# First expert tile's rows gathered into the tile of the diagonal's blocks, and a second list built in smaller pieces

## The chip, the cores and the metric

The kernel runs on one core of a Trainium2 chip. The metric is the device time of one launch in microseconds (us). Engines are named as in the profile: PE (TensorE's matmuls; PEld its weight loads), DVE (VectorE), ACT (ScalarE), POOL (GpSimd) and SP (the queue that starts most DMAs). Each engine works through its own queue in order, so a waiting instruction holds all that stand behind it.

## The reference

Attention without a softmax (the scaled scores pass through a relu and are squared), gated by u, is followed by a mixture of eight experts in which each token goes to its best one:

```python
B, S, D = 8, 2496, 256                   # d_qk = 64
scores = (1.0 / S) * np.matmul(z, z.transpose(0, 2, 1))
attn = np.maximum(scores, 0.0) ** 2
x = (u * np.matmul(attn, v)).reshape(B * S, D)
logits = x @ w_gate                      # E = 8
expert_idx = np.argmax(logits, axis=1)
probs = np.exp(logits - logits.max(-1, keepdims=True))
probs /= probs.sum(-1, keepdims=True) + 1e-09
gate_w = probs[np.arange(N), expert_idx]
for e in range(E):
    mask = expert_idx == e
    h = np.maximum(x[mask] @ w1[e], 0.0)     # F = 1024
    out[mask] = gate_w[mask, None] * (h @ w2[e])
```

## The kernel before

**Attention.** Eight batches of 2496 positions, each in five chunks of columns (four of 512, the last of 448), and each chunk in ten steps, `steps`. For a step, `scores()` makes two blocks of scores (it runs three steps ahead), and `weighted()` multiplies them with v into the chunk's accumulators. Values are carried as a high and a low part, which ACT and DVE make (`thi`, `tlo`). The matrix of scores is symmetric. Blocks on the diagonal go through a tile called `sd`, of which there is one; PE's transposes (line 298) are its last reads in a chunk. The last chunk of a batch (448 columns) doesn't use it.

**At a chunk's end.** `gate_x` multiplies with u and puts pieces on a list of background work, `bg`, of which one is issued at each following step (and later at each group of a tile): `logits` (its two small transposes `lg<-lp`, line 391, go out on SP), `turn_rows` (four transposes `rows<-th`, line 372, on SP, into a buffer of the ring `rows`, three deep), two empty turns, and then the three of `route`: `choose` (line 420 reads the transposed logits on DVE), `exps`, and `place`, which computes each token's place within its expert's list, stores the chunk's rows to memory (`xrows<-rows`, line 462) and scatters token numbers to the lists (`lst<-toks`, four indirect DMAs on POOL, line 467).

**Experts.** Tokens are handled in tiles of at most 512 rows, all of one expert. Six tiles (the list `la`, "A") hold tokens of the first seven batches and are known well before attention ends; the others (the list `lf`, "F") are made by `tile_list` after the last chunk, whose pieces stand on `bg` too. For each tile i: `load_w` fetches weights (POOL, line 672), `load_x` gathers the tile's rows, with a gate weight behind each row, by four indirect DMAs on POOL (line 681) into a buffer of the ring `rows`; `turn_x` transposes them by four DMAs on SP into `th` (line 712) and copies the four gate weights out, on DVE (line 714, `gt<-rows`); `split_x` makes the high and low parts, on ACT (lines 723 and 726) and DVE (724 and 727); `split_piece` does the same for the weights (lines 701 to 704). Then come 8 groups of a tile: `up` (line 744), a relu on ACT (line 748) and its low part on DVE (line 749), and `down` (lines 765 and 767), 14 matmuls in a full tile's group. `up` runs two groups ahead. In a tile's last group `finish` scales by the gate and scatters the rows out (lines 776 to 779). While tile i runs, the next ones are made ready: `load_x(i + 3)` at its first group, `turn_x(i + 2)` at its middle one, `split_x(i + 1)` three from its end.

**What sets the order.** A table, `loads`, says at which step, counted back from attention's last, the first tiles' loads, gathers and turnings are issued. A scheduler then orders each engine's queue by its own estimate of times; work issued through `pinned` stands behind the last instruction that each engine has been given so far. The table before:

```python
loads = {NKP + 4: [lambda: load_w(0, 0), lambda: load_w(0, 1)],
         NKP + 3: [lambda: load_x(0)],
         NKP - 1: [lambda: load_w(1, 0)],
         NKP - 4: [lambda: load_x(1)],
         NKP - 5: [lambda: turn_x(0)],
         1: [lambda: load_x(2)],
         0: [lambda: turn_x(1)]}          # NKP = 10
```

## Time and profile before

| | |
|---|---|
| runs | 2364.37, 2366.27, 2368.11 us (median 2366.27) |
| profiled execution | 2356.92 us, its span 2355.2 us |
| PE busy | 2303.9 us, 98% of the span |
| DVE busy | 1649.2 us, 70% |
| ACT busy | 1423.5 us, 60% |
| POOL busy | 641.6 us, 27% |

A row of the timeline gives the start, the duration, the engine, the line and what is written from what; in brackets stand the engine's idle time ahead of the row and what released it. "DMA rows<-xrows" as a releaser means that the engine waited for that transfer to land. A row of the windows gives, for a stretch, how long each engine was busy in it, the granted clock of PE (1.00 is full speed), and what the DMA engines did. Times are counted from the span's start. Attention ends and the experts begin near 1420 us.

### The profile page before, as it was taken

How to read it: one execution, taken by the hardware profiler on the slowest of the kernel's cores; microseconds unless marked ns; L12 is line 12 of the kernel's file. 1: busy time of each engine (PE TensorE's matmuls, PEld its weight loads, DVE VectorE, ACT ScalarE, POOL GpSimd, SP SyncE). 2: the span in 40 equal slices, each digit the busy share in tenths (PEclk: the TensorE clock that was granted, in tenths of full speed). 3: DMA queues.
4: the chain of work that ended last, by engine and by line, in shares of the span. 5: the costliest groups of instructions: out<-in, count | busy, mean ns of one | idle time of the engine just before them, and what ended most of it. 6: DMA issues, size and time to landing. Idle time of an engine off the chain costs nothing. (4 is left out here: it accounts for less than half of the span.)

```text
span 2355.2 us, 32513 instructions
## 1 busy us (share of the span) xinstructions
PE 2303.9 (98%) x11636; PEld 1937.7 (82%) x11636; DVE 1649.2 (70%) x3078; ACT 1423.5 (60%) x1944; POOL 641.6 (27%) x639
## 2 busy tenths in 40 slices
PE   8999999999999999999999988999999999999998
PEld 6888887888888888887888876788888888888887
DVE  8868868868868868868868846655666557557554
ACT  6757648658658648648658644355555556556443
POOL 4111111111111111111111225345445445346322
PEclk9999999999999999999999999999999999999999
DMA  5636637747647547547546767465657647557620
GB/s 136 102 65 120 114 62 121 109 68 133 103 69 139 88 78 135 91 74 131 98 75 115 126 114 130 115 150 166 170 140 193 148 133 198 149 147 190 148 87 28
DMA packets 424921, 280.16 MB, mean 119 GB/s; under 512 B 358380, under 2 KB 381690, under 8 KB 415536
## 3 DMA queue, kind: packets, MB, share of 16 engines
q1 hardware_dynamic: 393360, 158.91, 38.7%
q0 software_dynamic: 31392, 119.10, 18.5%
q8 instruction: 93, 1.52, 0.3%
q14 instruction: 76, 0.62, 0.1%
HBM read 149.79 MB, written 43.43 MB: 82 GB/s over the span
## 5 line engine op out<-in xcount | busy, mean ns | idle before, releaser
L332 PE MATMUL acc<-thi,t 128*128 128x512 f32 (+1 forms) x1600 | 619.9, 388 | 0.0
L329 PE MATMUL acc<-thi,t 128*128 128x512 f32 (+1 forms) x1600 | 595.7, 391 | 5.8 <-DVE thi L303 5.6
L331 PE MATMUL acc<-tlo,t 128*128 128x512 f32 (+1 forms) x1520 | 590.7, 389 | 4.3 <-DVE tlo L305 3.4
L765 PE MATMUL y<-t,t 128*128 128x512 f32 x1062 | 384.7, 399 | 4.5 <-ACT t L748 4.5
L749 DVE SCALAR_TENSOR_TENSOR t<-ph,t 128x512 fp32r<-128x512 f32 (+1 forms) x328 | 221.1, 675 | 235.0 <-ACT t L748 232.6
L744 PE MATMUL ph<-thi,t 128*128 128x512 f32 (+2 forms) x1248 | 379.9, 362 | 0.9 <-ACT thi L726 0.9
L467 POOL DMA_INDIRECT lst<-toks,posi x160 | 190.8, 1193 | 640.7 <-DVE posi L459 573.2
L748 ACT ACTIVATE t<-ph 128x512 fp32r<-128x512 f32 (+1 forms) x328 | 192.0, 588 | 279.6 <-PE ph L744 274.8
L329 PEld LDWEIGHTS acc<-thi,t 128*128 128x128 f32 x1600 | 300.9, 189 | 60.1 <-DVE thi L303 6.8
L332 PEld LDWEIGHTS acc<-thi,t 128*128 128x128 f32 x1600 | 301.8, 189 | 55.6
L331 PEld LDWEIGHTS acc<-tlo,t 128*128 128x128 f32 x1520 | 287.1, 189 | 58.7 <-DVE tlo L305 7.2
L767 PE MATMUL y<-t,t 128*128 128x256 f32 x1062 | 297.0, 283 | 10.8 <-DVE t L749 10.8
L744 PEld LDWEIGHTS ph<-thi,t 128*128 128x128 f32 x1248 | 227.3, 190 | 39.5 <-ACT thi L726 1.3
L765 PEld LDWEIGHTS y<-t,t 128*128 128x128 f32 x1062 | 200.8, 189 | 49.0 <-ACT t L748 4.9
L744 PE MATMUL ph<-tlo,t 128*128 128x512 f32 (+2 forms) x624 | 225.9, 362 | 0.8 <-DVE tlo L727 0.8
L767 PEld LDWEIGHTS y<-t,t 128*128 128x128 f32 x1062 | 202.3, 190 | 21.6 <-DVE t L749 12.6
L779 POOL DMA_INDIRECT out_dram<-tf,lfidx x136 | 143.3, 1054 | 276.5 <-DVE tf L777 246.6
L293 PE MATMUL ps_s<-t,t 128*128 128x512 f32 (+1 forms) x480 | 179.0, 377 | 0.0
L301 ACT ACTIVATE tf<-ps_s 128x1024 f32<-128x1024 f32 (+2 forms) x129 | 116.8, 906 | 92.2 <-PE ps_s L293 45.5
L681 POOL DMA_INDIRECT rows<-xrows,lfidx x136 | 141.3, 1039 | 44.1 <-issue 39.2
L303 DVE CAST thi<-tf 128x1024 fp32r<-128x1024 f32 (+2 forms) x129 | 85.1, 660 | 82.8 <-ACT tf L302 78.4
L267 DVE TENSOR_TENSOR tlo<-ps_s,thi 128x896 fp32r<-128x896 f32 (+1 forms) x80 | 89.1, 1114 | 61.4 <-ACT thi L266 60.9
(250 smaller groups left out, 3999.9 us busy)
## 6 DMA issues: line engine op xcount, KB each, us to landing
vr<-in_v_dram SPq DMA_DIRECT2D x80, 256.0 KB, 2.9
xrows<-rows SPq DMA_DIRECT2D x32, 544.0 KB, 3.9
u<-in_ut_dram SPq DMA_DIRECT2D x32, 512.0 KB, 4.5
zr<-in_zt_dram SPq DMA_DIRECT2D x40, 256.0 KB, 5.0
u<-in_ut_dram SPq DMA_DIRECT2D x8, 448.0 KB, 5.4
xrows<-rows SPq DMA_DIRECT2D x8, 408.0 KB, 3.6
rows<-th SPq DMA_TRANSPOSE x160, 4.7
lst<-toks,posi POOLq DMA_INDIRECT x160
```

The lines of the kernel that those rows point to most:

```text
L293: nc.tensor.matmul(ps[:, i, m:n], lhsT=hl_k, rhs=lh_q[:, m:n], start=False, stop=True)
L329: nc.tensor.matmul(acc[d][:, :n], lhsT=vh, rhs=hi[:, i, :n], start=first and i == 0, stop=False)
L331: nc.tensor.matmul(acc[d][:, :n], lhsT=vh, rhs=lo[:, i, :n], start=False, stop=False)
L332: nc.tensor.matmul(acc[d][:, :n], lhsT=vl, rhs=hi[:, i, :n], start=False, stop=last and i == 1)
L467: i = nc.gpsimd.indirect_dma_start(out=lst1, out_offset=bass.IndirectOffsetOnAxis(ap=posi[:m, j:j + 1], axis=0), in_=toks[:m, col + j:col ...
L681: nc.gpsimd.indirect_dma_start(out=xg[:, s, :], out_offset=None, in_=src, in_offset=bass.IndirectOffsetOnAxis(ap=lists[which]["idx"][:, s, ...
L744: nc.tensor.matmul(o, lhsT=w1[:, part, dd, fs], rhs=xx[:, dd, :n], start=p == 0, stop=p == 5)
L748: nc.scalar.activation(hh[:, :m], ph[:, :m], AF.Relu)
L749: nc.vector.scalar_tensor_tensor(hl[:, :m], ph[:, :m], 0.0, hh[:, :m].bitcast(F32), op0=ALU.max, op1=ALU.subtract)
L765: nc.tensor.matmul(y, lhsT=hh[:, cs], rhs=w2[:, f % 2].rearrange("p i d -> p (i d)"), start=f == 0, stop=False)
L767: nc.tensor.matmul(y[:, 0:D], lhsT=hl[:, cs], rhs=w2[:, f % 2, 0, :], start=False, stop=f == NF - 1)
L779: d = nc.gpsimd.indirect_dma_start(out=out, out_offset=bass.IndirectOffsetOnAxis(ap=lists[which]["idx"][:, s, t:t + 1], axis=0), in_=yo[:, ...
```

## The change

- The first tile's rows are gathered into the tile `sd`, which gets the shape of a `rows` buffer for that (`ring_sd`), in place of a buffer of the ring `rows`.
- `turn_x` loses the copy of the gates; that is a function of its own, `take_gates`.
- The table `loads` is new: tile 0 is gathered 12 steps from attention's end (13 before), tile 1 at 11 (6), tile 2 at 6 (1); tile 0 is turned at 9 (5) and tile 1 at 5 (0); their gates are copied at 7 and 3. All of these but the weights' pieces are `pinned`.
- Behind the last chunk's `turn_rows` stand four empty turns in place of two, so its `choose`, `exps` and `place` come two groups later.
- The second list is made in 15 pieces in place of 9; the first one's pieces stay as they were.
- In the tiles' loop the loads of weights are written under other conditions; POOL gets them in the order in which it got them.

```diff
+    def ring_sd():
+        return sb.tile([P, QC // P, ROW], I32, name="sd", tag="sd")
...
-            a = stored[b, c, c] = sb.tile([P, 2, QC], F32, name="sd", tag="sd")
+            sd = ring_sd().bitcast(F32).rearrange("p s r -> p (s r)")[:, 0:2 * QC]
+            a = stored[b, c, c] = sd.rearrange("p (i n) -> p i n", i=2)
...
-        bg.extend([nothing] * 2 + route(b * S + q0, n, ns, lg, xr))
+        bg.extend([nothing] * (4 if b == B - 1 and c == NC_ - 1 else 2) + route(b * S + q0, n, ns, lg, xr))
...
-        return r, [count] + ([middle, others] if ns else []) + [experts, rows, nothing, nothing, lambda: places(0), lambda: places(1)]
+        def all_of(*some):
+            return [lambda: [f() for f in some]]
+
+        if not ns:
+            return r, ([count] + all_of(lambda: experts(parts), experts2) + all_of(rows, rows2) + [nothing, nothing] +
+                       [lambda: places(0), lambda: places(1)])
+        nbig = t("nbig")
+        return r, [count, middle, middle2, lambda: others([(0, nd, 2 * BS, ndbl)]),
+                   lambda: others([(1, nb, BS, nbig)]), remaining, lambda: experts(parts[:2]),
+                   lambda: experts(parts[2:]), experts2, rows, rows2, nothing, nothing,
+                   lambda: places(0), lambda: places(1)]
...
-        xg = ring_rows()
+
+        xg = ring_sd() if i == 0 else ring_rows()
...
-        gates[i] = sb.tile([P, BS], F32, name="gt", bufs=4)
-        nc.vector.tensor_copy(gates[i][:, 0:k], xgs.pop(i)[:, 0:k, D].bitcast(F32))
-        turned[i] = tp
+        turned[i] = tp
+
+    def take_gates(i):
+        gates[i] = sb.tile([P, BS], F32, name="gt", bufs=4)
+        nc.vector.tensor_copy(gates[i][:, 0:blocks[i]], xgs.pop(i)[:, 0:blocks[i], D].bitcast(F32))
...
-             NKP + 3: [lambda: load_x(0)],
...
-             NKP - 5: [lambda: turn_x(0)],
-             1: [lambda: load_x(2)],
-             0: [lambda: turn_x(1)]}
+             NKP + 2: [lambda: load_x(0)],
+             NKP + 1: [lambda: load_x(1)],
+             NKP - 1: [lambda: load_w(1, 0), lambda: turn_x(0)],
+             NKP - 3: [lambda: take_gates(0)],
+             NKP - 4: [lambda: load_x(2)],
+             NKP - 5: [lambda: turn_x(1)],
+             NKP - 7: [lambda: take_gates(1)]}
...
-            f()
+            f() if f in plain else pinned(f)
...
-                for w, h in ((wof[i] + 1, 1), (wof[i] + 2, 0)):
-                    if own[i] and w <= wof[hi - 1]:
+                for w, h in ((wof[i] + 1, 0), (wof[i] + 1, 1), (wof[i] + 2, 0)):
+                    if own[i] and w <= wof[hi - 1] and (w, h) not in weights and (w < NA or i > NA):
...
                 turn_x(i + 2)
+                take_gates(i + 2)
```

Line numbers move: 681 becomes 706, 712 becomes 737, 714 is 742, 723 and 724 are 750 and 751, 744 is 771, 748 and 749 are 775 and 776, 462 is 466, 467 is 471, 391 is 395, 372 is 376, 420 is 424, 253 is 256, 267 is 270, 303 is 307, 388 is 392.

**VectorE at the last chunk's steps, before.** `gt` are the gate weights that are copied out, here tile 1's; `thi` and `tlo` are the two parts of scores or rows, line 702 is a weight's low part, and lines 388 and 389 write the logits of the chunk before.

```order
L267 TENSOR_TENSOR tlo<-ps_s,thi 128x2x448
L704 TENSOR_TENSOR t_13524<-s_13124,t_13524 128x2x256
L714 COPY gt<-rows 128x4
L702 TENSOR_TENSOR t_13552<-s_13124,t_13552 128x512
L267 TENSOR_TENSOR tlo<-ps_s,thi 128x2x448
L388 COPY lp<-lt 16x512
L389 COPY lp<-lt 16x512
```

**and now:**

```order
L270 TENSOR_TENSOR tlo<-ps_s,thi 128x2x448
L729 TENSOR_TENSOR t_13536<-s_13124,t_13536 128x2x256
L727 TENSOR_TENSOR t_13559<-s_13124,t_13559 128x512
L270 TENSOR_TENSOR tlo<-ps_s,thi 128x2x448
L742 COPY gt<-sd 128x4
L392 COPY lp<-lt 16x512
L393 COPY lp<-lt 16x512
L270 TENSOR_TENSOR tlo<-ps_s,thi 128x2x448
L372 COPY th<-x 128x1024
L729 TENSOR_TENSOR t_13560<-s_13124,t_13560 128x2x256
L751 COPY x<-th 128x1024
```

Tile 1's copy has left this place, and tile 0's, out of `sd`, has come to it from a place ahead of the last full chunk's split of the diagonal's block (lines 303 and 305). Tile 1's now stands further on, with tile 2's, around the reading of the logits of the chunk before the last:

```order
L313 TENSOR_TENSOR tlo<-tf,thi 128x448
L314 TENSOR_TENSOR thi<-tf,thi 64x448
L270 TENSOR_TENSOR tlo<-ps_s,thi 128x2x448
L742 COPY gt<-rows 128x4
L424 COPY lw<-lg 128x64 x2
L742 COPY gt<-rows 128x4
L727 TENSOR_TENSOR s_13775<-s_13318,s_13775 128x512
L729 TENSOR_TENSOR s_13775<-s_13318,s_13775 128x2x256
```

Tile 1's copy waits there with the reading of logits, and not ahead of it.

**VectorE in tile 0's and tile 1's groups, before.** Line 749 ends a group's relu (each has a number of its own), line 424 of now and 420 of before read the last chunk's logits, `x<-th` begins a tile's split.

```order
L714 COPY gt<-rows 128x4
L749 SCALAR_TENSOR_TENSOR t_13741<-ph,t_13740 128x512
L724 COPY x<-th 128x1024
L388 COPY lp<-lt 16x448
L389 COPY lp<-lt 16x448
L727 TENSOR_TENSOR tlo<-x,thi 128x1024
L749 SCALAR_TENSOR_TENSOR t_13760<-ph,t_13759 128x512
L420 COPY lw<-lg 128x64 x2
L422 TENSOR_TENSOR l<-lw 128x32
L749 SCALAR_TENSOR_TENSOR t_13806<-ph,t_13805 128x512
```

**and now:**

```order
L776 SCALAR_TENSOR_TENSOR t_13745<-ph,t_13744 128x512
L392 COPY lp<-lt 16x448
L393 COPY lp<-lt 16x448
L742 COPY gt<-rows 128x4
L751 COPY x<-th 128x1024
L776 SCALAR_TENSOR_TENSOR t_13764<-ph,t_13763 128x512
L754 TENSOR_TENSOR tlo<-x,thi 128x1024
L776 SCALAR_TENSOR_TENSOR t_13795<-ph,t_13794 128x512
L776 SCALAR_TENSOR_TENSOR t_13821<-ph,t_13820 128x512
L424 COPY lw<-lg 128x64 x2
L426 TENSOR_TENSOR l<-lw 128x32
```

The first copy here is tile 3's; the reading of the last chunk's logits stands two groups later than it did (after eight of the tiles' groups in place of six), and the copy one later (after five in place of four).

**SP, the last chunks' transfers, before.** `rows` are a chunk's rows or a tile's, `lg` the logits; x7 counts transposes in a row.

```order
L372 DMA_TRANSPOSE rows<-th 128x4x128 x4
L462 DMA xrows<-rows 128x4x272
L141 DMA u<-in_ut_dram 128x2x448
L712 DMA_TRANSPOSE th<-rows 128x4x128
L391 DMA_TRANSPOSE lg<-lp 128x4x16 x2
L372 DMA_TRANSPOSE rows<-th 128x4x128 x4
L712 DMA_TRANSPOSE th<-rows 128x4x128 x7
L462 DMA xrows<-rows 128x4x272
L712 DMA_TRANSPOSE th<-rows 128x4x128 x7
L391 DMA_TRANSPOSE lg<-lp 128x4x16 x2
```

**and now:**

```order
L376 DMA_TRANSPOSE rows<-th 128x4x128 x4
L466 DMA xrows<-rows 128x4x272
L737 DMA_TRANSPOSE th<-sd 128x4x128 x4
L144 DMA u<-in_ut_dram 128x2x448
L395 DMA_TRANSPOSE lg<-lp 128x4x16 x2
L376 DMA_TRANSPOSE rows<-th 128x4x128 x4
L737 DMA_TRANSPOSE th<-rows 128x4x128 x4
L466 DMA xrows<-rows 128x4x272
L737 DMA_TRANSPOSE th<-rows 128x4x128 x5
L395 DMA_TRANSPOSE lg<-lp 128x4x16 x2
L376 DMA_TRANSPOSE rows<-th 128x4x128 x4
```

Tile 0's four transposes have moved ahead of the fetch of u, and tile 1's ahead of the second store. Ahead of the last chunk's logits stand five transposes of tiles where there were seven.

## Rows read from the trace of the kernel before

**Rows 1.** The page's head.

```profile
span 2355.2 us, 32513 instructions
```

**Rows 2.** Windows: us; busy PE, PEld, DVE, ACT, POOL; clock, DMA, GB/s.

```profile
1360.00:1560.00 200.00, 174.22 (x842) 144.53 (x841) 114.84 (x315) 82.93 (x129) 80.96 (x78) 0.93 0.65 135
1500.00:1540.00 40.00, 40.00 (x202) 33.35 (x201) 23.07 (x58) 16.28 (x32) 23.64 (x23) 1.00 0.65 191
1560.00:2300.00 740.00, 738.45 (x4000) 639.26 (x3999) 450.15 (x767) 413.23 (x730) 327.38 (x312) 1.00 0.57 153
```

**Rows 3.** Windows behind four idle pieces of PE.

```profile
1405.25:1410.50 5.25, 5.25 (x14) 4.69 (x15) 4.79 (x8) 1.87 (x2) 1.15 (x1) 0.50 0.59 184
1424.20:1427.60 3.40, 3.40 (x9) 2.65 (x9) 1.74 (x5) 1.24 (x2) 1.65 (x3) 0.50 0.37 95
1455.30:1461.70 6.40, 6.37 (x22) 5.10 (x23) 5.92 (x26) 4.50 (x7) 3.27 (x4) 0.50 0.65 159
1482.40:1485.60 3.20, 3.20 (x10) 2.67 (x11) 3.17 (x14) 3.20 (x6) 0.00 (x0) 0.50 0.00 0
```

**Rows 4.** Timeline of PE: rows with idle time ahead of them.

```profile
1366.18 0.49 PE L329 MATMUL acc<-thi,t 128*128 128x512 f32 x1 [1.09 <-DVE thi L303]
...
1405.25 0.74 PE L292 MATMUL ps_s<-t 128*128 128x448 f32 x1 [6.92 <-DVE tlo L267]
...
1422.71 0.51 PE L744 MATMUL ph<-thi,t 128*128 128x512 f32 x1 [0.95 <-ACT thi L726]
...
1423.97 0.65 PE L744 MATMUL ph<-tlo,t 128*128 128x512 f32 x1 [0.75 <-DVE tlo L727]
...
1443.43 0.39 PE L767 MATMUL y<-t,t 128*128 128x256 f32 x1 [1.33 <-DVE t L749]
...
1455.33 0.58 PE L767 MATMUL y<-t,t 128*128 128x256 f32 x1 [5.42 <-DVE t L749]
...
1482.38 1.22 PE L765 MATMUL y<-t,t 128*128 128x512 f32 x2 [4.48 <-ACT t L748]
...
1547.61 0.58 PE L767 MATMUL y<-t,t 128*128 128x256 f32 x1 [3.69 <-DVE t L749]
```

**Rows 5.** Timeline of DVE: copies of gates and reads of logits.

```profile
1365.30 0.17 DVE L714 COPY gt<-rows 128x4 f32<-128x4 f32 x1 [10.75 <-DMA rows<-xrows,laidx]
...
1403.43 0.17 DVE L714 COPY gt<-rows 128x4 f32<-128x4 f32 x1 [12.83 <-DMA rows<-xrows,laidx]
...
1416.48 0.30 DVE L420 COPY lw<-lg 128x64 uint16<-128x64 uint16 x2
...
1442.62 0.17 DVE L714 COPY gt<-rows 128x4 f32<-128x4 f32 x1 [6.64 <-DMA rows<-xrows,laidx]
...
1453.49 0.21 DVE L420 COPY lw<-lg 128x64 uint16<-128x64 uint16 x1 [6.46 <-DMA lg<-lp]
```

**Rows 6.** Timeline of ACT: the splits of tiles 5 and 7.

```profile
1480.54 1.34 ACT L723 COPY x<-th 128x1024 uint16<-128x1024 uint16 x1 [9.62 <-DMA th<-rows]
...
1546.22 1.35 ACT L723 COPY x<-th 128x1024 uint16<-128x1024 uint16 x1 [7.42 <-DMA th<-rows]
```

**Rows 7.** Timeline of POOL: gathers, tile 1's last and tile 3's first.

```profile
1394.27 0.94 POOL L681 DMA_INDIRECT rows<-xrows,laidx  x1 [0.30 <-issue]
...
1432.46 1.06 POOL L681 DMA_INDIRECT rows<-xrows,laidx  x1 [6.30 <-DVE pos L455]
```

**Rows 8.** Timeline of SP's queue near the last chunk's end.

```profile
1428.49 0.39 SPq L462 DMA_DIRECT2D xrows<-rows  x1
...
1429.05 11.84 SPq L712 DMA_TRANSPOSE th<-rows  x7
...
1444.33 4.14 SPq L391 DMA_TRANSPOSE lg<-lp  x2
```

**Rows 9.** Timeline of PE: the last transposes out of sd.

```profile
1364.49 0.60 PE L298 MATMUL ps_s<-ident,sd 128*128 128x128 f32 x4
```

More of the change, by code (lines that the diff above doesn't have):

```diff
@@ L168, in fused_kernel @@
                             pattern=[[1, P]], channel_multiplier=-1)
-    raw = sb.tile([P, 2, QC], F32, name="sd", tag="sd").rearrange("p i n -> p (i n)").bitcast(I32)
+    raw = ring_sd().rearrange("p s r -> p (s r)")
     used = [0]
@@ L540, in count @@
             nc.vector.scalar_tensor_tensor(units, done, -float(2 * BS), units, op0=ALU.mult, op1=ALU.add)
+        if ns:
+            want, ctake, take = t("want", (P, 2, E)), t("ctake", (P, 2 * E)), t("take", (P, 2, E))
         def middle():
-            want, ctake, take = t("want", (P, 2, E)), t("ctake", (P, 2 * E)), t("take", (P, 2, E))
             half = t("half")
@@ L556, in middle, with others @@
             nc.vector.scalar_tensor_tensor(units, take[:, 0, :], -3.0, units, op0=ALU.mult, op1=ALU.add)
-        def others():
-            full, nbig = t("full"), t("nbig")
-            for w, n, blocks_, number in ((0, nd, 2 * BS, ndbl), (1, nb, BS, nbig)):
+        def others(which):
+            for w, n, blocks_, number in which:
+                full = t("full")
                 floor_shift(full, units, blocks_.bit_length() - 1, "fi")
@@ L581, in tile_list, with experts @@
                 parts.append((a, a + n, w))
-        def experts():
-            for a, z, w in parts:
+        def experts(some):
+            for a, z, w in some:
                 s3 = [P, z - a, E]
@@ L800, in fused_kernel @@
     loads = {NKP + 4: [lambda: load_w(0, 0), lambda: load_w(0, 1)],
[L801 to L806 removed]
+             NKP + 2: [lambda: load_x(0)],
[5 more added lines that the diff above has]
+             NKP - 7: [lambda: take_gates(1)]}
     for q in range(LP + 1):
         loads.setdefault(LP - q, []).append(lambda q=q: split_piece(q))
+    plain = [loads[LP - q][-1] for q in range(LP + 1)]
     for s, (b, c, kp) in enumerate(steps):
@@ L912, in more @@
         turn_x(lo + 1)
+        take_gates(lo)
+        take_gates(lo + 1)
         split_x(lo)
```

6 lines of the change are left out of this document (4 added, 2 removed).

## The prediction

> **What bounds the kernel now.** I read the span first, then its stretches, then TensorE's (PE) own waits, then the engine and the queue behind each wait. The profiled execution's span is 2355.2 us [rows 1]. In [rows 2], PE is busy 738.45 of 740 us from 1560 us on, but only 174.22 of 200 us between 1360 and 1560, where attention ends and the experts begin: 25.78 us idle at a mean granted clock of 0.93. [Rows 3] give a second price: right behind four of the idle pieces the clock stands at 0.50, which is the 1.2 GHz level. A stretch at half clock loses half its length: 5.25, 3.40, 6.40 and 3.20 us lose 2.6, 1.7, 3.2 and 1.6 us. So the program is PE's work plus what this stretch leaves idle. An instruction saved on another engine is worth nothing unless PE waits for it.
>
> [Rows 4] are PE's idle pieces, each in brackets with what released it. I name them in order of time: A 1.09 (1366.18), B 6.92 (1405.25), C 0.95 and 0.75 (1422.71 and 1423.97), D 1.33 (1443.43), F 5.42 (1455.33), G 4.48 (1482.38), H 3.69 (1547.61). These are 24.63; the 1.15 left of 25.78 lies in two short pieces right behind A and D, and I put 0.76 to A and 0.39 to D. With the half clock (H, which has no row of its own, priced as G): A 1.85, B 9.5, C 3.4, D 1.7, F 8.6, G 6.1, H 5.3: together 36.5 us, all that this change could reach.
>
> The releasers are engines that themselves stood still. VectorE (DVE) held its in-order queue at a 0.17 us copy of gates, line 714, for 10.75 us (A), 12.83 us (B) and 6.64 us (D), waiting for a gather to land; at line 420 it waited 6.46 us for the transposed logits (F) [rows 5]. ScalarE (ACT) stood at line 723 for 9.62 us (G) and 7.42 us (H), waiting for the transposed rows of a tile [rows 6]. PE's loss is the wait less the work that stood ready: 9.62 − 4.48 = 5.1 us and 7.42 − 3.69 = 3.7 us of cover.
>
> **The change part by part.**
>
> *Gate copies.* Each copy leaves the transposes and gets a place of its own. Tile 0's moves from ahead of the last full chunks' split (line 303) to between two late splits, some 35 us on; its gathers then lie far back, so A's wait goes, 1.85 us. Tile 1's moves from 1390.6 (1403.43 − 12.83) to where the logits of the chunk before the last are read. That reading began at 1416.48 [rows 5]; without A and B it comes 11.4 us sooner, at 1405.1. Tile 2's copy now stands beside it, and takes over the gathers that ended B: tile 2's take tile 1's old place on POOL, ending about 1.85 us before 1395.2 [rows 7], and should land by 1403.43 − 1.85 = 1401.6. That is 3.5 us ahead of need, so I book no wait for it; bounds: nothing to 3 us. B goes, 9.5 us.
>
> *Tile 0's gathers into the diagonal's tile.* Eight gathers now run back to back, where four ran early and four late. They may start when PE has read the diagonal's blocks for the last time, the transposes of 1364.49 that last 0.60 [rows 9]: 1365.1. POOL takes 0.94 us and 0.31 between, 1.25 us each [rows 7]: tile 0's leave by 1370, tile 1's by 1375. The nearest landing is 1403.43 − 1395.21 = 8.2 us behind the last gather, so tile 0 is there by 1378. Ahead of that I see nobody hurt: POOL's next work behind them are the list scatters of a chunk whose places are not yet computed then. On SP, tile 0's four transposes now stand ahead of a fetch of u. A transpose took 11.84 / 7 = 1.69 us [rows 8]; the four take 6.8 us, against a u that attention reads only where the last chunk ends. The cost is nothing, against the bound of 6.8 us if that fetch were late. Tile 0's split then no longer waits for its transposed rows, and C goes, 3.4 us. The first expert matmul comes at 1422.71 less A, B and C's first piece: 1422.71 − 1.85 − 9.5 − 0.95 = 1410.4.
>
> *The tile side.* The clock of the tiles starts 12.3 us sooner, so what must be compared is demand against supply. Demand: 40 us hold 202 matmuls [rows 2], a group has 14, so it lasts 2.77 us. Supply: tile 3's gathers wait for a rows buffer that the store of the chunk before the last gives back; 1432.46 − 1428.49 = 4.0 us lie between them [rows 7, 8]. That store follows attention's DVE queue and moves from 1428.49 to about 1414.4 with A, B and the tail of C. The gathers then start at 1418.4, and from the first to the gate copy it took 1442.62 − 1432.46 = 10.2 us: 1428.6. The copy stands after 5 groups instead of 4, at about 1410.4 + 6 × 2.77 = 1427. D comes to nearly nothing (0 to 2.5). F: seven transposes stood ahead of the last chunk's logits on SP, for 11.84 us from 1429.05, so that these were issued at 1444.33 [rows 8]. Now tile 0's and 1's are long done and five stand there; the logits go out at about 1424, and DVE reads them after 8 groups instead of 6, at about 1410.4 + 8 × 2.77 = 1432.6. They needed 1453.49 − 1444.33 = 9.2 us, so they arrive at 1433. F is gone, 8.6 us (bound: 3 us left).
>
> A new wait, S. Tile 3's last three transposes stand behind the two of the logits (4.14 us [rows 8]) and four of the chunk's rows (4 × 1.69 = 6.8): 1424 + 10.9 + 3 × 1.69 = 1440, undisturbed. But the logits' pair, with gathers under way, took 9.2 us where its issue took 4.14, so they may land 5 us later, 1445. ACT and DVE reach tile 3's split after ten groups, 1410.4 + 27.7 = 1438.1. The wait is 2 to 7 us, up to 10 if the rows' transposes stand still as well, and the cover 3.7 to 5.1: PE idles 0 to 6. I take 2.6, between, and C's 1.7 of half clock: 4.3.
>
> G: tile 5's transposes follow tile 4's, and the chain ahead of them starts 14 us sooner against a demand 12 to 15 us sooner (S included); with F's delay of list and store gone, the wait shrinks from 9.62 to about the cover. I book 0.5 (0 to 7). H: tile 7 comes from the second list. Cutting its making into 15 pieces in place of 9, and two empty turns ahead of the last chunk's routing, puts its last write one group later (29 groups ahead to 30) and tile 7's split two groups later (35 to 37). The pieces hold the same instructions, so they cost DVE nothing more. One more gather stands ahead on POOL (1.25 us); 3.69 − 2.77 + 1.25 = 2.2 us idle, and 1.4 of half clock: 3.6.
>
> **The sum.** Left over: 4.3 + 0.5 + 3.6 = 8.4 us, and 0.3 for D's edge. Gain 36.5 − 8.7 = 27.8. The profiled execution, 2356.92 us, would become 2329.1; the median of the runs shown, 2366.27, lies 9.4 above it, and I carry the gain over to it: 2338.5 us.
>
> A rule speaks about S. The logits' transposes stood still beside gathers: 9.2 us against 4.14 [rows 5, 8]. The Trainium skill, "DMA: Bandwidth & Descriptors", section "Queues, rings and completion order", says that a DMA engine takes turns between its queues packet by packet, so that a queue of gathers would not shut out a queue of transposes. By that rule S would be near nothing and the time 2334; this trace rather speaks against it, though it does not show which packets stood ahead.
>
> **The rivals.**
> 1. *Transposes and gathers share the queues evenly.* S's wait then ends at 1440, inside the cover, and 4.3 us more are gained: 2334. Against it: the 9.2 us. 12%.
> 2. *Only attention's side gains.* A, B and C (14.8 us) hang on copies that stood in the wrong place, and go; but the tile side is paced by a chain (last chunk's logits, routing, second list, gathers, transposes), and if that chain moves no more than PE's demand, then D, F, G and H reappear one place on, 21.7 us: 2366.3 − 14.8 = 2351.5. For it: every wait there ends on a DMA whose chain starts at the same chunk ends. Against it: F's two extra groups and the shorter SP queue come on top. 20%.
> 3. *The waits only move.* Tile 2's gathers land as late after their issue as tile 0's transposes are held up, and B comes back at the new copies, some 9.5 us, with rival 2's leftovers: 2361, to 2366. Against: 3.5 us of slack. 5%.
> 4. *Slower: the eight gathers are held.* They wait for the diagonal's tile, and they stand in POOL's and SP's queues in one row: if its release or POOL comes late, tile 0 comes late, and all of PE waits for tile 0 at attention's end. From the start of the gathers to the split's end: 5.0 + 8.2 + 6.8 + 3 for the split = 23 us, so starts up to 1410.4 − 23 = 1387 are free; each us behind that is one us of PE idle. Held to attention's end they cost 23 us idle and 2.6 of half clock, with C's 3.4 and the tile side kept: −11.4 + 25.6 = +14, 2380. It breaks even, with the tile side kept, when they start at about 1398. Against it: the last reader of the diagonal's tile ends at 1365.1, 22 us ahead of the point from which it costs. 4%.
>
> **How the numbers follow.** The forecast, 2330 (nothing left of 36.5) to 2350 (S 6 and 1.7, G 7 and H as before are 20.0 of it), has 59%; the rivals have 12, 20, 5 and 4. About 0.2%, 4.7 us, is what a measurement of this kernel can tell from no change. Forecast and rivals 1 and 2 are faster (91%, of which I give 3 away for mixtures that I have not seen); rival 3 is half same; rival 4 has some starts that come out even: faster 0.88, same 0.07, slower 0.05. The likeliest time is 2338.5. The range runs from 2329 (all of 36.5 gone, less 1 for the measurement) to 2355, which takes in rival 2 and leaves out rivals 3 and 4.
>
> **What would show it.** In the changed kernel's trace: no wait over 1 us at the gate copies (A, B, D right; else rival 3); PE without a piece near 1405, and the first expert matmul near 1410; the gathers into the diagonal's tile at 1365 to 1370 (after 1387: rival 4); SP issuing the last chunk's logits by 1426 and DVE reading them without a wait over 2 us (F); ACT waiting 5 to 10 us at tile 3's split with 1 to 6 us of PE idle behind it (S; without it, rival 1); tile 5's split without PE idle (G; else rival 2); tile 7's with about 2 us (H). PE idle from 1360 to 1560 should fall from 25.78 to about 6 us. The prediction is wrong if that idle stays above 15 us, or if the span differs by more than that idle and its half clock say.

## The result

The changed kernel takes 2339.68 us (median of 4 runs, 2330.73 to 2344.18), the kernel before 2365.32 us beside it. The medians' quotient is 0.9892; the ratio on record for the runs together is 0.99, with a 95% interval of 0.9874 to 0.9926. The forecast was 2338.5 us, 0.9883 of the median it started from. Two more comparisons, each on a chip with the kernel before beside it, gave 2345.21 against 2356.52 (0.9948, 0.9931 to 0.9965) and 2327.5 against 2354.85 (0.989, 0.9869 to 0.9911): gains of 25.6, 11.3 and 27.4 us. The forecast's size, 27.8 us, is that of two of the three. The first traces of both kernels are of executions faster than the median (2330.73 us here, 2356.92 before), so what makes other executions of the same kernel slower is not in them.

The profiled execution of the changed kernel has a span of 2329.0 us, 26.2 below [rows 1], and the stretch of [rows 2] reads now (length, then busy PE, PEld, DVE, ACT and POOL, clock, DMA share, GB/s):

```profile
span 2329.0 us, 32511 instructions
```

```profile
1360.00:1560.00 200.00, 188.15 (x961) 157.77 (x960) 124.55 (x331) 96.13 (x151) 91.72 (x92) 0.97 0.72 150
1560.00:2300.00 740.00, 740.00 (x4012) 641.78 (x4011) 450.43 (x769) 413.11 (x731) 326.47 (x310) 1.00 0.55 150
```

PE's idle time from 1360 to 1560 us has fallen from 25.78 to 11.85 us, and the mean granted clock has risen from 0.93 to 0.97. PE's rows of this execution, the first matmul of the experts and then the idle pieces:

```profile
1406.68 0.39 PE L771 MATMUL ph<-thi,t 128*128 128x512 f32 x1
...
1408.79 0.50 PE L771 MATMUL ph<-thi,t 128*128 128x512 f32 x1 [0.56 <-DVE x L357]
...
1427.33 0.38 PE L794 MATMUL y<-t,t 128*128 128x256 f32 x1 [0.27 <-DVE t L776]
...
1442.94 0.80 PE L771 MATMUL ph<-thi,t 128*128 128x512 f32 x1 [5.66 <-DVE t L776]
...
1446.43 0.50 PE L771 MATMUL ph<-thi,t 128*128 128x512 f32 x1 [0.56 <-DVE t L776]
...
1528.52 1.22 PE L792 MATMUL y<-t,t 128*128 128x512 f32 x2 [2.68 <-ACT t L775]
...
1531.82 0.58 PE L794 MATMUL y<-t,t 128*128 128x256 f32 x1 [2.08 <-DVE t L776]
```

Against [rows 4]: A, B and C are gone; a small new piece, 0.56 us at 1408.79, waits for the last chunk's product with u (line 357). D is 0.27 us, F and G are gone, tile 3's new wait S stands at 1442.94 and 1446.43 with 6.22 us, and H at 1528.52 and 1531.82 with 4.76. VectorE's rows show which wait is where:

```profile
1389.29 0.16 DVE L742 COPY gt<-sd 128x4 f32<-128x4 f32 x1
...
1402.65 0.16 DVE L742 COPY gt<-rows 128x4 f32<-128x4 f32 x1
...
1403.59 0.17 DVE L742 COPY gt<-rows 128x4 f32<-128x4 f32 x1
...
1425.70 0.17 DVE L742 COPY gt<-rows 128x4 f32<-128x4 f32 x1 [5.38 <-DMA rows<-xrows,laidx]
...
1430.22 0.30 DVE L424 COPY lw<-lg 128x64 uint16<-128x64 uint16 x2
...
1441.57 0.74 DVE L751 COPY x<-th 128x1024 uint16<-128x1024 uint16 x1 [8.85 <-DMA th<-rows]
...
1519.40 0.36 DVE L742 COPY gt<-rows 128x4 f32<-128x4 f32 x1 [5.41 <-DMA rows<-xrows,lfidx]
```

The copies of tiles 0, 1 and 2 (lines 742, at 1389.29, 1402.65 and 1403.59) wait for nothing, where those of [rows 5] stood 10.75 and 12.83 us. Tile 3's waits 5.38 us, which costs PE 0.27. The last chunk's logits (line 424 at 1430.22) are there when VectorE comes, where it stood 6.46 us. New are 8.85 us ahead of tile 3's split (1441.57) and 5.41 at tile 7's copy (1519.40). On ScalarE and on SP's queue:

```profile
1441.55 1.33 ACT L750 COPY x<-th 128x1024 uint16<-128x1024 uint16 x1 [7.48 <-DMA th<-rows]
...
1525.56 1.33 ACT L750 COPY x<-th 128x1024 uint16<-128x1024 uint16 x1 [10.57 <-DMA th<-rows]
```

```profile
1422.77 1.22 SPq L395 DMA_TRANSPOSE lg<-lp  x1
...
1425.36 1.22 SPq L376 DMA_TRANSPOSE rows<-th  x1
...
1432.24 1.21 SPq L737 DMA_TRANSPOSE th<-rows  x1
```

Tile 3's split waits 7.48 us, tile 5's 1.96 (9.62 before [rows 6]), tile 7's 10.57 (7.42 before). The logits go out at 1422.77, 21.6 us sooner than in [rows 8], and behind them stand the chunk's four transposes (6.78 us) and then tile 3's.

To compare executions on several chips, two intervals are worked out from each trace. The first runs from the last transposes out of the tile of the diagonal's blocks ([rows 9] in the kernel before), up to which the kernels are the same, to the experts' first matmul: the attention side. The second runs from there to the relu of the 57th group, behind which nothing is changed: the tile side. In microseconds:

| kernel (trace) | attention side | tile side | both |
|---|---|---|---|
| before | 58.2 | 180.6 | 238.8 |
| before, second trace | 58.4 | 188.7 | 247.2 |
| changed | 44.7 | 172.5 | 217.2 |
| changed, second | 46.5 | 182.4 | 228.9 |
| changed, third | 44.7 | 168.9 | 213.6 |
| gates' copies alone | 50.6 | 185.6 | 236.1 |
| copies back in the turning | 44.7 | 174.7 | 219.3 |
| tile 0 in the ring of rows | 44.7 | 188.5 | 233.2 |
| two empty turns | 44.7 | 188.1 | 232.8 |
| nine pieces | 46.4 | 173.6 | 220.0 |
| tile 3 in the diagonal's tile | 44.7 | 182.7 | 227.4 |
| list first | 46.4 | 178.4 | 224.8 |
| list first, second | 45.1 | 165.6 | 210.7 |
| both, with late copies | 45.4 | 181.0 | 226.4 |

The attention side repeats within 2 us for one kernel, the tile side within 14 (13.5 for the changed kernel, 8.1 for the one before). A difference of a few microseconds on the tile side of two traces is therefore not yet the work of an edit.

### The profile page after: what moved, and what is told of

Read it like the earlier page. It is cut to its first block, busy times and chain, and to the rows that moved or that the text cites. A ratio compares the mean times of both kernels' runs of the same rounds, so it can differ in the third digit from the quotient of the medians.

```text
span 2329.0 us, 32511 instructions
## 1 busy us (share of the span) xinstructions
PE 2292.9 (98%) x11636; PEld 1930.7 (83%) x11636; DVE 1649.6 (71%) x3078; ACT 1425.7 (61%) x1944; POOL 641.1 (28%) x639
## 4 chain that ended last, share of the span: by engine, by line
PE 91%; DMA 4%; issue 1%; ACT 1%; DVE 1%; SPq 1%; POOL 0%; POOLq 0%; DVEq 0%; ACTq 0%
PE ph L771 17%; PE acc L336 15%; PE acc L333 14%; PE acc L335 14%; PE y L792 12%; PE y L794 6%; PE ps_s L296 4%; PE ps_s L297 4%; PE ps_s L268 3%; DMA vr<-in_v_dram 1%; PE pt L383 1%; DMA th<-rows 1%; PE ps_s L302 1%; DMA lg<-lp 1%; DMA rows<-xrows,lfidx 1%
## 5 line engine op out<-in xcount | busy, mean ns | idle before, releaser
L333 PEld LDWEIGHTS acc<-thi,t 128*128 128x128 f32 x1600 | 300.1, 188 | 58.3 <-DVE thi L307 5.0
L792 PEld LDWEIGHTS y<-t,t 128*128 128x128 f32 x1062 | 199.6, 188 | 46.5 <-ACT t L775 3.1
L305 ACT ACTIVATE tf<-ps_s 128x1024 f32<-128x1024 f32 (+2 forms) x129 | 116.9, 907 | 74.3 <-DVE tlo L304 35.8
```

The lines of the kernel that those rows point to most:

```text
L333: nc.tensor.matmul(acc[d][:, :n], lhsT=vh, rhs=hi[:, i, :n], start=first and i == 0, stop=False)
L792: nc.tensor.matmul(y, lhsT=hh[:, cs], rhs=w2[:, f % 2].rearrange("p i d -> p (i d)"), start=f == 0, stop=False)
```

## The experiments

The runs came in three groups of four, each group on one chip with the kernel before beside it (2356.52, 2371.38 and 2354.85 us). Only within a group are times compared. The second group has no run of the changed kernel, so its edits are compared with the changed kernel by traces alone.

### The changed kernel again

No edit.

> The changed kernel once more, as the measure for the runs beside it and for its own spread (2330.73 to 2344.18 in four runs). If the waits that are left (tile 3's split, 5.66 us of PE idle, and tile 7's, 4.76) hang on when transfers land, they differ between executions: the median near 2339, single runs 2329 to 2345. If the spread was a matter of the first runs alone, they agree within 5 us.

Measured: 2345.21 us (2339.34 to 2347.34), ratio 0.9948. Its attention side is that of the first trace within 2 us; what is longer is the tile side. There, from 1520.6 to 1534.6, PE idles 11.5 us in a way of which neither the kernel before's first trace nor the changed one's has anything. Two windows of 10 us, two of PE's rows in the first of them, and ScalarE's row behind them:

```profile
1520.00:1530.00 10.00, 2.37 (x9) 1.29 (x7) 0.17 (x1) 0.00 (x0) 7.75 (x8) 0.65 0.99 246
1530.00:1540.00 10.00, 6.13 (x17) 4.97 (x17) 4.11 (x6) 4.83 (x6) 0.97 (x1) 0.50 0.83 162
```

```profile
1523.83 0.59 PE L792 MATMUL y<-t,t 128*128 128x512 f32 x1 [1.95 <-issue]
...
1529.58 0.59 PE L771 MATMUL ph<-thi,t 128*128 128x512 f32 x1 [2.59 <-issue]
...
1531.05 0.60 ACT L775 ACTIVATE t<-ph 128x512 fp32r<-128x512 f32 x1 [13.09 <-remote]
```

PE is busy 2.37 of 10 us, and its rows, one matmul every 2 to 3 us, wait for "issue": for nothing that the profile shows. The group of matmuls had begun; ScalarE stands idle for 13.09 us until its next relu, released by "remote", that is by no instruction and no transfer that the profile knows. POOL goes on at its usual pace (7.75 us busy of 10). A smaller stretch of the kind stands ahead of tile 3: a relu of ScalarE at 1436.72 waits 7.67 us for "remote", and PE 0.72 for "issue" and 2.85 for that relu. The wait S at tile 3 itself is 0.98 us here, since the split is reached that much later. The two branches of the expectation are both half right: the idle time at tiles 3 and 7 differs between executions, but the larger part of what this trace lost to the first is of this other kind.

> The changed kernel a third time, as the measure for the three beside it. Against the kernel before it gained 25.6 us in the first comparison and 11.3 in the second; by my steps it should gain 20 to 28, and less only where an execution loses time at tile 7's place in which PE waits for nothing that the trace shows (14 us of such time stand in the second trace). If that is so, the gain here lies between 11 and 28, and the trace's share of it at attention's side (A, B, C) is the same as in the first.

Measured, on a third chip: 2327.5 us (2322.6 to 2333.68), ratio 0.989, interval 0.9869 to 0.9911. Its PE rows have idle pieces at tile 3 and tile 7 alone:

```profile
1436.10 0.80 PE L771 MATMUL ph<-thi,t 128*128 128x512 f32 x1 [4.05 <-DVE t L776]
...
1439.58 0.50 PE L771 MATMUL ph<-thi,t 128*128 128x512 f32 x1 [0.55 <-DVE t L776]
...
1521.23 0.73 PE L792 MATMUL y<-t,t 128*128 128x512 f32 x2 [2.08 <-ACT t L775]
...
1524.04 0.39 PE L794 MATMUL y<-t,t 128*128 128x256 f32 x1 [2.08 <-DVE t L776]
```

S is 4.60 us and H 4.16 here, and no row waits for "issue". So the gain is 26 to 27 us where the traces are free of such stretches, and it was 11 where one stood in the changed kernel's trace. That the stretch is the whole difference isn't shown: there is no trace of the kernel before from that chip.

### The kernel before again

No edit.

> The kernel before once more, with a trace from the same chip as the runs beside it. In the first comparison it stood at 2365.3 us and the changed kernel 25.6 below it, in the second at 2356.5 and 11.3 below. Theory: the attention side's waits A, B and C and the tile side's F are in every execution, and about 25 us of idle time stand between 1360 and 1560 us again; what differs is the start and tile 7's place. Rival: on this chip the gathers land sooner, and the waits at the copies of the gates are half as long.

Measured: 2370.75 us, ratio 0.9999 (0.9984 to 1.0014) to the same kernel's runs beside it, so the comparison itself is sound to 0.15%. The pieces up to G are those of [rows 4] in other sizes, with one of 2.14 us at 1471.80 beside them; at tile 7's place PE waits 5.07 us for "issue". Two of the pieces:

```profile
1406.84 0.74 PE L292 MATMUL ps_s<-t 128*128 128x448 f32 x1 [5.42 <-DVE tlo L267]
...
1455.96 0.58 PE L767 MATMUL y<-t,t 128*128 128x256 f32 x1 [7.17 <-DVE t L749]
```

B is 5.42 (6.92) and F 7.17 (5.42); the attention side is 58.4 us where it was 58.2. The theory holds for that side: it doesn't hang on the chip. The rival is out: the copies stand 11.94 and 11.26 us, where it was 10.75 and 12.83.

### The copies of the gates alone

```diff
 # the kernel before, with
...
+    gate_at = {NKP - 7: 0, 0: 1}
...
+        if LAST - s in gate_at:
+            pinned(lambda: take_gates(gate_at[LAST - s]))
...
                 turn_x(i + 2)
+                take_gates(i + 2)
```

> The kernel before with nothing changed but the place of the copies of the gates (tile 0's seven steps from attention's end, tile 1's and 2's at its end, on POOL and SP the order of before). Theory: A and B were the copies' waits, so 11.4 us go: 2366 - 11.4 = about 2355; the waits of the tile side (D to H) stay, and C stays, since tile 0 is transposed as late as before. Rival: the copies only showed that the gathers were late; with the gathers where they were, the waits come back at tile 0's split or tile 2's copy, and at most 3 us are gained: 2363 to 2366.

Measured: 2351.22 us against 2356.52, ratio 0.9979 (0.9969 to 0.999): 5.3 us and not 11.4. The attention side went from 58.3 to 50.6 us. A and B are gone, but a piece that was 0.95 us in [rows 4] now reads:

```profile
1410.40 0.80 PE L746 MATMUL ph<-thi,t 128*128 128x512 f32 x1 [5.74 <-ACT thi L728]
```

The experts' first matmul waits 5.74 us for tile 0's split. With A and B gone, PE comes to it 12.5 us sooner (counted from the common point), and tile 0's transposed rows are not sooner by as much. The theory's A and B were right, its "C stays" was not: C grows from 0.95 to 5.74 us and takes 4.8 of the 12.5 back. In the changed kernel, whose tile 0 is gathered and turned early as well, C is gone.

### The copies back in the turning

```diff
         turned[i] = tp
-
-    def take_gates(i):
         gates[i] = sb.tile([P, BS], F32, name="gt", bufs=4)
...
-             NKP - 3: [lambda: take_gates(0)],
-             NKP - 7: [lambda: take_gates(1)]}
```

> The changed kernel with the copy of a tile's gates back in the turning of its rows; gathers, the tile of the diagonal's blocks, empty turns and pieces as changed. Theory: what removed A and B is that the copies stand behind their gathers' landing; with tiles 0 to 2 gathered 12, 11 and 6 steps from attention's end the scheduler puts the copies at the same places in VectorE's queue, so A and B stay gone: within 3 us of the changed kernel. Rival: a function of its own for the copy is what does it; the copies hold VectorE again and 5 to 10 us are lost.

Measured: 2330.24 us against 2327.5 of the changed kernel beside it (0.9904, 0.9881 to 0.9928, against 0.989, 0.9869 to 0.9911): the same within the intervals, and an attention side of 44.7 us in both. The function of its own does nothing that can be measured. The copies have not gone back to their old places, though, since the turnings are earlier too: tile 0's stands 20.3 us behind the common point, where the changed kernel has it at 27.3 and the kernel before at 0.8; tile 1's stands at 37.0, where VectorE came to it at 26.1 in the kernel before. A's copy had to move in any case, since VectorE came to it 9.9 us ahead of the point from which the diagonal's tile can be filled. For B, early gathers alone would do by an estimate: tile 1's leave by 11.1 us behind the common point, and with the 8.2 us that a landing took in the kernel before they are there by 19.3. That later copies alone take A and B away as well, but not C, is shown by the run before this one.

### Tile 0 in the ring of rows

```diff
-        xg = ring_sd() if i == 0 else ring_rows()
+        xg = ring_rows()
```

> The changed kernel with tile 0's rows gathered into the ring of rows, as before, in place of the tile of the diagonal's blocks; all else as changed. Theory: tiles 0 and 1 then hold two of the ring's three buffers over the last two chunks, the chunks' stores and tile 2's gathers wait for them, and B or a like wait comes back: 8 to 15 us slower than the changed kernel. Rival: the third buffer is enough, and the tile of the diagonal's blocks was needed for nothing: within 3 us of the changed kernel.

Measured: 2352.17 us, ratio 0.9925 (0.9896 to 0.9955). The changed kernel's ratios are 0.989 to 0.9948 on other chips, so the time alone doesn't decide; the trace says where this kernel waits. VectorE's row, and PE's:

```profile
1409.22 0.17 DVE L742 COPY gt<-rows 128x4 f32<-128x4 f32 x1 [4.91 <-DMA rows<-xrows,laidx]
```

```profile
1411.91 0.50 PE L771 MATMUL ph<-tlo,t 128*128 128x512 f32 x1 [2.46 <-DVE tlo L754]
```

Tile 2's copy of the gates waits 4.91 us for its gather, which in this order of POOL comes behind three loads of weights, the last of which stood 5.83 us itself; tile 0's split stands behind that copy on VectorE, and PE idles 2.46 us. That is what the forecast's third rival describes, B at the new place, in a kernel without the extra buffer. A and B themselves don't come back (attention side 44.7 us), so the theory's 8 to 15 us aren't shown; about 5 at this place are: the ninth relu comes 73.6 us behind the common point, where it comes 68.2 and 66.9 in the changed kernel's first and third trace (in the second, 76.2, the relu that waits for "remote" stands ahead of it). That the gathers stand later for want of a buffer isn't shown by a wait: POOL stands 0.30 us ahead of the first of them, and it is the order that differs. The rest of this trace's long tile side lies at tile 7's place, 4.09 us of "issue" and 9.26 behind a relu that waits 12.04 us for "remote", which is not this edit's.

### Two empty turns

```diff
-        bg.extend([nothing] * (4 if b == B - 1 and c == NC_ - 1 else 2) + route(b * S + q0, n, ns, lg, xr))
+        bg.extend([nothing] * 2 + route(b * S + q0, n, ns, lg, xr))
```

> The changed kernel with two empty turns behind the last chunk's pieces in place of four, so that VectorE reads the last chunk's logits after six groups and not eight. Theory: the logits land near 1428 to 1430, six groups are over at about 1427, so VectorE waits about 3 us more than now, and the second list comes two groups sooner: the wait F comes back as 0 to 4 us, and H is shorter by about as much, within 4 us of the changed kernel. Rival: F's 8.6 us were the two groups' doing alone: 6 to 9 us slower.

Measured: 2355.8 us, ratio 0.9936 (0.9911 to 0.9961). VectorE does not wait at the last chunk's logits, but just ahead of them it stands 6.89 us at tile 3's copy, under which a wait for them could lie; PE loses 2.16 us there, D's place, where the changed kernel loses 0.27. F has no piece of its own. But PE idles 10.64 us at tile 3, and SP's queue and its waits from 1436 to 1446 show a part of why:

```profile
1432.77 0.38 PE L794 MATMUL y<-t,t 128*128 128x256 f32 x1 [2.16 <-DVE t L776]
...
1457.29 0.79 PE L771 MATMUL ph<-thi,t 128*128 128x512 f32 x1 [10.64 <-DVE t L776]
```

```profile
1438.77 1.22 SPq L737 DMA_TRANSPOSE th<-rows  x1
...
1443.88 0.36 SPq L466 DMA_DIRECT2D xrows<-rows  x1
...
1444.90 1.25 SPq L737 DMA_TRANSPOSE th<-rows  x1
```

```profile
SPq L466 <- DMA rows<-th: 3.7, 2, 3.1
```

With the routing two groups sooner, the scheduler puts the last chunk's two stores (1443.88 and 1444.29) ahead of tile 3's last two transposes, and the first of them waits until 1443.88: SP stands from 1439.99 on, 3.7 us of it for the chunk's own transposed rows to land. Tile 3's transposes follow at 1444.90, and ScalarE's split of it waited 11.03 us. Both theory and rival fall in their reason: F does not come back as a piece of its own, but a store that waits gets in the queue ahead of a tile's transposes. The price is S, 10.6 us of idle where the changed kernel has 6.2 and 4.6, and the 2.16 us ahead of it. Counted from the common point, tile 3's second transpose goes out 3.6 us later than in the changed kernel and its third 8.4: the two stores, with SP's standing, are the difference. A relu of ScalarE that waits 4.82 us for "remote" lies in between as well, so the stores are not the whole.

### Nine pieces

```diff
-        return r, [count, middle, middle2, lambda: others([(0, nd, 2 * BS, ndbl)]),
-                   lambda: others([(1, nb, BS, nbig)]), remaining, lambda: experts(parts[:2]),
-                   lambda: experts(parts[2:]), experts2, rows, rows2, nothing, nothing,
-                   lambda: places(0), lambda: places(1)]
+        return r, ([count] + all_of(middle, middle2) +
+                   all_of(lambda: others([(0, nd, 2 * BS, ndbl), (1, nb, BS, nbig)]), remaining) +
+                   all_of(lambda: experts(parts), experts2) + all_of(rows, rows2) + [nothing, nothing] +
+                   [lambda: places(0), lambda: places(1)])
```

> The changed kernel with the second list made in 9 pieces, as before. Theory: the list is ready at the same group (its last write stands behind 30 groups in either), and the pieces hold the same instructions, so nothing is lost or gained: within 3 us of the changed kernel. Rival: larger pieces hold VectorE in a row, so that relus' low parts come late and PE waits, 3 to 8 us slower.

Measured: 2330.79 us, 0.9891 (0.9872 to 0.991), beside 2327.5, 0.989: the same. The pieces' number is worth nothing that these times show, as forecast. The two traces differ by 6.4 us in the table, 3.4 of it at tile 7 (7.54 us of idle against 4.16), but the changed kernel's is of an execution 4 us below its median and this one's of one 1 us above.

### Tile 3 in the diagonal's tile

```diff
-        xg = ring_sd() if i == 0 else ring_rows()
+        xg = ring_sd() if i in (0, 3) else ring_rows()
```

> The changed kernel with tile 3's rows, too, gathered into the tile of the diagonal's blocks, which is free again once tile 0 is transposed and its gates are copied, so that they need not wait for the store of the chunk before the last. Theory: tile 3's wait S (5.66 and 0.56 us of PE idle and some 1.7 of half clock) comes from its transposes standing behind the last chunk's; gathered early they stand ahead, and 6 to 8 us go: about 2332 against 2339.5. Rival: what the transposes of tile 3 are spared, those of tile 4 or the logits' have to wait, and the idle time turns up one tile on: within 2 us of the changed kernel.

Measured: 2345.93 us beside the changed kernel's 2345.21: no gain. VectorE's row and PE's tell the price:

```profile
1408.23 0.17 DVE L742 COPY gt<-sd 128x4 f32<-128x4 f32 x1 [5.15 <-DMA sd<-xrows,laidx]
```

```profile
1410.89 0.80 PE L771 MATMUL ph<-tlo,t 128*128 128x512 f32 x1 [4.20 <-DVE tlo L754]
...
1450.46 0.50 PE L771 MATMUL ph<-thi,t 128*128 128x512 f32 x1 [4.29 <-DVE t L776]
```

The scheduler moved tile 3's copy of the gates ahead of tile 0's split, where it stood 5.15 us, and PE 4.20; and a wait of 4.29 us turned up further on, where tile 4 is split. At tile 3's split ScalarE waits only 0.71 us, so the theory was right that early gathers take S away from there. The rival's time came out; its reason is shown in part: the copy's 4.20 us are the edit's, but tile 4's split, which waits 2.08 us, stands behind a relu that waits 7.48 us for "remote".

### Both, with late copies

```diff
 # tile 3 in the diagonal's tile, the list's reads ahead of the weights, and
-                take_gates(i + 2)
+                pinned(lambda: take_gates(i + 2))
```

> Tile 3's rows into the tile of the diagonal's blocks, as in the run where VectorE then stood 5.15 us at tile 3's copy of the gates, but with the copies of the tiles' gates issued no earlier than where they are written, and the second list's reads ahead of the weights of the F tiles. Theory: S (about 6 us) goes without the new wait, and part of H: 6 to 12 us below the changed kernel, 2333 to 2339 where that stands at 2345. Rival: the gates' copies then give the buffers back too late and gathers wait for them: the same as the changed kernel or slower.

Measured: 2407.1 us, ratio 1.016 (1.0131 to 1.0189), 36 us slower than the kernel before. The rival was right. In the view of one tile, the gates' (who waited for it, us, times), and in that of PE's waits:

```profile
  POOL rows L710: 89.7, 15
```

```profile
PE ph L775 <- DVE t L780: 32.4, 12, 8.4
```

The gathers waited 89.7 us for copies to give their buffers back, all through the experts, and PE 32.4 for the relus' low parts. So the loss lies behind the table's end: 814 us pass from the 57th relu to the span's end, where it is 750 to 762 in the other kernels. A copy too early holds VectorE; one too late holds the ring.

### List first

```diff
...
+        with ExitStack() as behind:
+            if NA <= w <= wof[NM - 1]:
+                behind.enter_context(tc.issue_after(lists[which]["read"]))
             nc.gpsimd.indirect_dma_start(out=wr, out_offset=None, in_=wcat,
```

> The changed kernel with the reads of the second list put ahead of the weights of the F tiles on POOL (three loads of weights stand ahead of them there). Theory: H (2.68 and 2.08 us of PE idle and half clock behind) is the chain from those reads to tile 7's gathers and transposes; it starts 3.8 us sooner on POOL and its landing no longer stands behind three large loads: 5 to 7 us go, about 2333.5. Rival: the weights then come late, and the splits of the first F tile's weights hold VectorE: no gain, or up to 5 us slower.

Measured: 2340.14 us (0.9921, 0.9899 to 0.9942) beside 2345.21 (0.9948, 0.9931 to 0.9965): lower by 5 us, with intervals that overlap, so a gain isn't shown.

> Once more the changed kernel with the second list's reads ahead of the F tiles' weights; it stood 5 us below the changed kernel in one comparison, with intervals that touch. Theory: 3 to 7 us below the changed kernel. Rival: that was chance, within 2 us.

Measured: 2329.96 us (0.9894, 0.9876 to 0.9912) beside 2327.5 (0.989, 0.9869 to 0.9911). No gain that the times show. The trace has what the edit is for: POOL's rows of the changed kernel and of this one, the last scatter of the lists' tokens being long over in both:

```profile
1483.53 0.99 POOL L696 DMA_INDIRECT s<-in_wcat_dram,lfwidx  x1 [12.45 <-issue]
...
1487.35 1.12 POOL L637 DMA_INDIRECT vr<-lst,lflidx  x1 [0.30 <-DVE t L776]
```

```profile
1478.52 0.95 POOL L637 DMA_INDIRECT vr<-lst,lflidx  x1 [11.15 <-DVE lflidx L633]
```

```profile
1514.94 0.38 PE L798 MATMUL y<-t,t 128*128 128x256 f32 x1 [2.01 <-DVE t L780]
```

The reads go out first instead of fourth, and H is 2.01 us of idle where the changed kernel has 4.16 on the same chip. Of a span of 2320 us, 2 us are under what the runs tell apart (they spread over 8 to 11).

## Why the prediction was right, step by step

**Attention side (A, B, C).** Forecast: the first matmul of the experts at 1410.4, which is 45.9 us behind the common point; measured 44.7, 46.5 and 44.7, where it was 58.2 and 58.4. This step stands as worked out, with the gathers where it put them (the first into the diagonal's tile at 1363.69, forecast 1365.1):

```profile
1363.69 0.98 POOL L706 DMA_INDIRECT sd<-xrows,laidx  x1 [12.64 <-ACT thi L303]
```

One link of it was wrong in its weight: moving the copies was booked as what frees B. The experiments show that the copies alone give about 8 of the 13 us, because C grows; with tile 0 gathered and turned early all 13 come, and it doesn't matter whether the copy is written as part of the turning.

**D and F.** Forecast nearly nothing and nothing; measured 0.27 and nothing, the logits issued at 1422.77 (forecast 1424) and read at 1430.22 (forecast 1432.6). F's two causes can't be kept apart as the prediction did: with two empty turns PE has no piece behind the logits either, but it loses 2.16 us behind tile 3's copy, under which a wait for them could lie; what the turns are worth is seen at tile 3. The logits' pair also landed sooner than was taken, 4.9 us behind its issue at 1422.77 and not 9.2. The second of the pair, issued at 1424.05, took 3.6 us to land:

```profile
DMA to landing us min/median/max: 3.6/3.6/3.6
```

**S.** The new wait is there, at the place that was given, but PE's idle time is mis-sized: 2.6 us of idle and 1.7 of half clock were taken; measured 6.22 us in the first trace and 4.60 in the third, inside the 0 to 6 that was allowed, or just past it. The term that was wrong is the cover. ScalarE waited 7.48 us, and 5.87 in the third trace, of the 2 to 7 (10) forecast:

```profile
1434.71 1.34 ACT L750 COPY x<-th 128x1024 uint16<-128x1024 uint16 x1 [5.87 <-DMA th<-rows]
```

PE idled 5.66 and 4.05 of that in its first piece, so the work that stood ready was 1.8 us in both, and not the 3.7 to 5.1 that were taken over from G and H. The sum's reason for the wait, transposes that land late beside gathers, is less sure. Counted from the common point, the rows were there for ScalarE at 79.5 us in the first trace and 76.7 in the third, where the first rival's 1440 is 75.5 and the forecast's 1445 is 80.5; and ScalarE came to the split at 72.1 and 70.8, ahead of the 73.6 that were taken. So the rival's time, 2334 with S near nothing, is out, while its supply is missed by 4.0 us in one trace and 1.2 in the other. The rule of the Trainium skill, "DMA: Bandwidth & Descriptors", section "Queues, rings and completion order", by which a DMA engine takes turns between its queues, is not decided here. While ScalarE waited, from 1432 to 1441.5, both queues moved (SP's is the first row: packets, MB, share of 16 engines):

```profile
q1 hardware_dynamic: 3300, 0.80, 62.0%
q0 software_dynamic: 164, 0.45, 41.3%
```

The engines were full, so turns and long waits can stand side by side; no row shows whose packets went ahead.

**G.** Forecast 0.5 us, measured none; tile 5's split waits 1.96 us, under its cover.

**H.** Forecast 2.2 us of idle; measured 4.76 and 4.16. The step that failed is the 2.77 us that the sum took off for a demand one group later. In the order it came as forecast: the second list is read behind 26 groups' relus in place of 25, and tile 7 is split behind 37 in place of 35. In time it did not. The list's first read before, and VectorE's second split in the changed kernel:

```profile
1510.40 0.94 POOL L623 DMA_INDIRECT vr<-lst,lflidx  x1 [0.30 <-issue]
```

```profile
1530.45 0.74 DVE L751 COPY x<-th 128x1024 uint16<-128x1024 uint16 x1 [1.22 <-DMA th<-rows]
```

Before, ScalarE came to tile 7's split 28.4 us behind that read, and its rows were there 35.8 us behind it. In the changed kernel, whose read is at 1487.35, it is 27.6 and 38.2 (27.7 and 37.8 in the third trace): a demand no later, and a supply later by 2 to 2.4 us, where 1.25 were added. So the wait grew from 7.42 to 10.57 us, of which the cover left 2.68. Why the group doesn't show in time stays open. The other 2.08 us are a piece that the sum didn't have: PE waits for a relu that stands behind VectorE's split of the next tile, which itself waited 1.22 us. VectorE's copy of tile 7's gates, 5.41 us, cost PE nothing in the first trace and 0.22 us in the third.

**The sum.** Of 27.8 us, 12.3 were booked to the attention side and 15.5 to the tile side. The traces give 13.0 (58.3 to 45.3, means of two and three traces) and 10.0 (184.6 to 174.6): 23, with the stretches of the last section in the second trace of either kernel. In the first pair it is 13.5 and 8.1, to which come 2.5 us that the changed kernel's execution is ahead already at the common point and 2.1 behind the 57th group, neither of them the change's doing as far as the code shows. PE's idle time from 1360 to 1560 fell to 11.85 us, under the 15 at which the prediction called itself wrong, but twice the 6 that it named. So the span came out at 2329.0, where the forecast for it was 2329.1 less 1.7 around it, by some luck: S and H were 6 us too small (3.6 and 2.6 of idle), and about 5 us of the measured gain lie outside the changed stretch.

**The rivals.** The second (only the attention side gains) has its time in the second trace, where the tile side is 182.4 us, as before, but not its reason: D, F, G and H haven't come back there, "issue" and "remote" have come instead. In the first and third it is out. The third, waits that move, shows itself in kernels that are one edit away (tile 2's copy without the extra buffer, tile 3's copy with it used twice), not in this one. The fourth, gathers held, is out: they started at 1363.69, 23 us ahead of the point from which they would cost.

## What to carry to other kernels

A copy of a few words out of a gather can hold a whole in-order engine: look for the small instruction with a wait of 10 us ahead of it, and start the transfer earlier rather than move the copy, for the next consumer of the same transfer is late as well (here C, 0.95 to 5.74 us). When a stretch ahead is shortened, ask for each wait behind it whether its supply moves with the demand, and don't take the work that stood ready at one wait for that at another (here 1.8 us, where 3.7 to 5.1 were taken). A store that waits for its data held the transposes behind it on SP for 3.9 us, and two empty turns kept it out of the way.

## What was not expected of the hardware

All eight traces of the first two groups have rows of PE between 1430 and 1546 us that wait 0.5 us or more for "issue", one to seven of them, 1.1 to 12.2 us in all, whatever the kernel; the four of the third group and the first traces of both kernels have none. The same eight, and no other, have rows of ScalarE between 1430 and 1550 us that wait for "remote", the longest in each 4.8 to 13.1 us. All fourteen traces hold 11636 matmuls, so lost rows are not the reason. The waits go with the chip, or with something else that differed between the groups, as far as fourteen traces tell, and they fall on one kernel more than on another: the changed kernel has 12.2 us of them in one trace and none in two. POOL and the DMA engines worked on in the longest stretch (DMA share 0.99 in the window from 1520). The queue that loads instructions moved little there between 1500 and 1545: in the trace with the stretch (packets, MB, share of 16 engines) it has the row below, in the first one without it 0.1%.

```profile
q8 instruction: 2, 0.03, 0.3%
```

What holds PE and ScalarE there stays open; no run took the weights' loads or the gathers out of that stretch to see whether it goes.
